# Reordering the opening of a fused linear-attention and feed-forward kernel: FFN1 of the first tokens from the first weight slice on, FFN2 of the first tokens in weight order

## The chip, the cores and the metric

The kernel runs on one core of one Trainium2 chip. The metric is device time in microseconds (us), as the median of several executions. A profile records one execution. Its span, from the first to the last instruction, is 1.7 to 2.9 us shorter than the time of the same execution. Times inside a profile count from the start of that span.

Engines: TensorE (PE in the profile; PEld is its weight loads), VectorE (DVE), ScalarE (ACT), GpSimd (POOL), and SyncE (SP), whose queue (SPq) issues the DMAs. In the traces ScalarE, VectorE and GpSimd take up their instructions in the order in which the program issues them.

## The reference

```python
# attention: B=4, H=8, S=768, D=48
for t in range(S):
    cur = einsum('bhd,bhe->bhde', u[None] * kt, vt)
    y[:, :, t] = einsum('bhd,bhde->bhe', rt, state + cur)
    state = w[None, :, :, None] * state + einsum('bhd,bhe->bhde', kt, vt)
# feed-forward on x = y as 3072 tokens x 384
h = maximum(x @ w_in, 0)          # 384 -> 2048
out = (h * h) @ w_out             # 2048 -> 384
```

## The kernel before

The sequence is cut into 24 chunks of 128 tokens, four batches times six. Two chunks make a group g of 256 tokens, so there are 12 groups. A chunk i passes through these pieces:

- `prep(i)`: scale k and r by decay powers (two products, into `rk`). `prep_du(i)`: two products for the bonus term.
- `turn(i)`: transpose `rk` into `rkT`. Chunks 0 to 3 do it on TensorE with a ScalarE copy, later chunks by a DMA transpose.
- `piece_A` (scores on TensorE, masked by VectorE into `Bm`), `bonus` (VectorE: `du`, then the product `dv`), `piece_YU` (output Y and state increment U, then state update `S0W`), `piece_X` (transpose into `xT`, the FFN input).

A group then passes through FFN1 in eight pieces s (`piece_F1`: one slice of `w_in`, relu, square) and FFN2 in eight pieces (`piece_F2`). In the steady state one period runs `piece_F1(g, s)`, `piece_F2(g-1, s)` and the attention of group g+1, woven over s = 0 to 7.

```python
    def piece_F1(g, s):
        xT = xTs[g]
        hp = psH.tile([128, 2, GT], FP32, name=f"hp_{g}_{s}", tag="H")   # psH: two buffers
        ...                                                            # six matmuls with W1[s]
        nc.scalar.activation(hr, hp, AF.Relu)
        if s % 4 == 3:
            nc.scalar.activation(hq, hr, AF.Square)
        else:
            nc.vector.tensor_mul(hq, hp, hr)          # frees hp only here

    def att(g, s):
        a = 2 * g
        b = a + 1
        if s == 0:   cast_v(a); piece_A(a); bonus(a)
        elif s == 2: cast_v(b); piece_A(b); bonus(b)
        elif s == 3: piece_YU(a)
        elif s == 4: piece_YU(b)
        elif s == 5: piece_X(a)
        elif s == 6: piece_X(b)

    def preps(g, s):
        if s == 0:   prep(2 * g, nc.gpsimd); turn(2 * g)
        elif s == 2: prep_du(2 * g, nc.gpsimd)
        elif s == 4: prep(2 * g + 1, nc.gpsimd); turn(2 * g + 1)
        elif s == 6: prep_du(2 * g + 1, nc.gpsimd)
    # (att and preps: line breaks shortened)

    for i in range(4):                        # the opening
        prep(i, nc.vector)
        prep_du(i, nc.gpsimd)
        turn(i)
        if i % 2 == 1:
            period(i // 2, None, None)        # attention of groups 0 and 1
    for s in range(NS):
        cast_w1(s)                            # all weight casts on GpSimd
    for s in range(NS):
        cast_w2(s)
    ...                                       # preps of chunks 4 and 5, loads
    period(None, 0, None)                     # FFN1 of group 0
    period(None, 1, None)                     # FFN1 of group 1
    period(2, None, 0)                        # attention of group 2 with FFN2 of group 0
    for g in range(2, NG + 1):
        period(g + 1 if g + 1 < NG else None, g if g < NG else None, g - 1)
```

## Time and profile before

| | kernel before |
|---|---|
| time, three runs | 205.73 us (205.68 to 205.82) |
| span of the profile | 203.6 us |
| first FFN1 matmul of group 0 / of group 2 | 32.8 / 61.3 us |
| periods with attention, group 3 on (mean of eight) | 13.7 us |
| last group without attention, then the FFN2 left over | 10.4 and 5.2 us |

The timeline of TensorE: start, duration (both in us), engine, line, operation, output and inputs, shape, number of instructions merged.

```profile
32.76 1.49 PE L319 MATMUL hp_0_497<-xT_315,W_0_439 128*128 128x256 bf16 x6
34.04 1.49 PE L319 MATMUL hp_1_508<-xT_315,W_1_441 128*128 128x256 bf16 x6
35.66 0.90 PE L319 MATMUL hp_2_519<-xT_315,W_2_443 128*128 128x256 bf16 x6
...
61.26 0.82 PE L319 MATMUL hp_0_832<-xT_795,W_0_439 128*128 128x256 bf16 x6
```

Six matmuls of FFN1 make one piece `hp`. The first two pieces take 1.49 us from first start to last end and the third takes 0.90. The last line shown is where the steady state begins.

The table of waits of TensorE between 61 and 184 us: who waited for whom, the sum, how often, the longest.

```profile
PE Ap_1396 L251 <- DMA rkT_1250<-rk_182: 0.9, 1, 0.9
PE Ap_1890 L251 <- DMA rkT_1744<-rk_182: 0.8, 1, 0.8
...
PE Ap_1149 L251 <- DMA rkT_1003<-rk_178: 0.5, 1, 0.5
```

There are seven such waits, each in a period of its own. TensorE stands still until the DMA transpose of the group's second chunk has landed.

Busy time by engine in four periods of the steady state (the window, its length, then PE, PEld, DVE, ACT and POOL in us with instruction counts, the granted clock, and the DMA share and rate). Each window runs from one group's first FFN1 matmul to the next.

```profile
core 0: us, PE busy (x) PEld busy (x) DVE busy (x) ACT busy (x) POOL busy (x), PEclk, DMA share, GB/s
88.15:102.13 13.98, 13.03 (x136) 9.59 (x134) 10.59 (x18) 8.43 (x17) 9.96 (x11) 1.00 0.69 152
102.13:115.84 13.71, 13.03 (x136) 9.60 (x134) 10.32 (x18) 8.43 (x17) 9.51 (x11) 1.00 0.70 154
115.84:129.73 13.89, 13.05 (x136) 9.59 (x134) 10.50 (x18) 8.43 (x17) 9.94 (x11) 1.00 0.75 141
129.73:143.38 13.65, 12.99 (x136) 9.60 (x134) 10.26 (x18) 8.44 (x17) 9.51 (x11) 1.00 0.83 159
```

### The profile page before, as it was taken

What the parts mean: (1) busy time and instruction counts of PE and PEld (TensorE: products, weight loads), DVE (VectorE), ACT (ScalarE), POOL (GpSimd) and SP (SyncE); (2) the same over time, 40 slices, a digit from 0 to 9 for tenths busy, and PEclk for the clock granted to TensorE, in tenths of its full rate; (3) what the DMA queues carried; (4) which work ended last, traced back from release to release, by engine and by line L of the source; (5) the groups of instructions that cost most, each with busy time, mean ns of one, the idle gap of its engine ahead of it and who ended that gap; (6) DMA issues with size and microseconds to landing.
All of it is one profiled execution on the core that took longest, in us unless ns stands there. A gap on an engine that the chain in (4) does not pass through costs nothing.

```text
span 203.6 us, 4241 instructions
## 1 busy us (share of the span) xinstructions
PE 168.7 (83%) x1624; PEld 123.2 (61%) x1624; DVE 133.2 (65%) x230; ACT 109.9 (54%) x203; POOL 117.8 (58%) x130
## 2 busy tenths in 40 slices
PE   0763647677959998998999989989989899999992
PEld 0643434455546776775767757767767577677761
DVE  4379793454966939849759489397595783963310
ACT  3360613657516484575574745755756657556640
POOL 2487973891856494692992965938929749100000
PEclk9999999999999999999999999999999999999999
DMA  5999999829714946929929649689499396311112
GB/s 109 208 209 279 384 351 252 223 52 192 146 40 94 207 118 142 197 77 194 219 54 210 152 109 214 96 176 207 60 210 180 92 210 120 84 42 39 39 40 79
DMA packets 105140, 31.07 MB, mean 153 GB/s; under 512 B 96672, under 2 KB 105120, under 8 KB 105120
## 3 DMA queue, kind: packets, MB, share of 16 engines
q1 hardware_dynamic: 105120, 30.81, 66.3%
q8 instruction: 12, 0.20, 0.4%
q14 instruction: 8, 0.07, 0.1%
HBM read 20.84 MB, written 4.72 MB: 126 GB/s over the span
## 4 chain that ended last, share of the span: by engine, by line
PE 25%; POOL 24%; DVE 20%; DMA 13%; SPq 8%; issue 5%; ACT 4%; ACTq 0%
SPq L83 2%; SPq L81 2%; DMA kf_1562<-in_k_dram 2%; DMA kf_2056<-in_k_dram 2%; DMA kf_1315<-in_k_dram 2%; DMA kf_1809<-in_k_dram 2%; DMA kf_1068<-in_k_dram 2%; DMA rf_110<-in_r_dram 2%; DMA vf_828<-in_v_dram 2%; POOL rk_180 L199 1%; POOL rk_178 L199 1%; POOL rk_182 L200 1%; POOL rk_178 L200 1%; POOL S0W_211 L298 1%; POOL rk_182 L199 1%
## 5 line engine op out<-in xcount | busy, mean ns | idle before, releaser
L319 PEld LDWEIGHTS <-W_0_439 128*128 128x128 bf16 x72 | 7.3, 102 | 3.0 <-issue 0.9
L319 PEld LDWEIGHTS <-W_2_443 128*128 128x128 bf16 x72 | 7.1, 99 | 3.3 <-issue 1.3
L182 PE MATMUL wl_ps<-esel,wrow 1*128 1x96 f32 x16 | 3.7, 423 | 6.5 <-ACT wrow L174 6.5
L319 PEld LDWEIGHTS <-W_6_451 128*128 128x128 bf16 x72 | 6.6, 97 | 2.6 <-issue 1.9
L319 PEld LDWEIGHTS <-W_3_445 128*128 128x128 bf16 x72 | 6.4, 97 | 2.9 <-issue 1.2
L319 PEld LDWEIGHTS <-W_4_447 128*128 128x128 bf16 x72 | 6.5, 97 | 2.4 <-issue 1.7
L319 PEld LDWEIGHTS <-W_1_441 128*128 128x128 bf16 x72 | 6.6, 102 | 2.0
L182 PEld LDWEIGHTS wl_ps<-esel,wrow 1*128 1x128 f32 x16 | 3.5, 325 | 6.5 <-ACT wrow L174 6.5
L319 PEld LDWEIGHTS <-W_7_453 128*128 128x128 bf16 x72 | 6.7, 98 | 0.7
L319 PEld LDWEIGHTS <-W_5_449 128*128 128x128 bf16 x72 | 6.5, 98 | 0.7
L199 POOL TENSOR_TENSOR rk_180<-kf_486,Wkhat 128x384 bf16<-128x384 f32 x1 | 1.0, 1007 | 4.9 <-DMA kf_486<-in_k_dram 4.9
L309 ACT COPY xT_315<-px_316 128x384 bf16<-128x384 bf16 x1 | 0.5, 479 | 6.2 <-PE px_316 L308 6.2
L309 ACT COPY xT_428<-px_429 128x384 bf16<-128x384 bf16 x1 | 0.5, 479 | 6.0 <-PE px_429 L308 6.0
L205 POOL TENSOR_TENSOR P_0_215<-rf_90,kf_91 128x384 f32<-128x384 f32 x1 | 1.4, 1366 | 4.0 <-DMA kf_91<-in_k_dram 4.0
L199 POOL TENSOR_TENSOR rk_176<-kf_821,Wkhat 128x384 bf16<-128x384 f32 x1 | 1.0, 998 | 4.6 <-DMA kf_821<-in_k_dram 4.6
L199 POOL TENSOR_TENSOR rk_180<-kf_1068,Wkhat 128x384 bf16<-128x384 f32 x1 | 1.0, 999 | 4.1 <-DMA kf_1068<-in_k_dram 4.1
L199 POOL TENSOR_TENSOR rk_180<-kf_1562,Wkhat 128x384 bf16<-128x384 f32 x1 | 1.0, 1007 | 4.0 <-DMA kf_1562<-in_k_dram 4.0
L199 POOL TENSOR_TENSOR rk_180<-kf_2550,Wkhat 128x384 bf16<-128x384 f32 x1 | 1.0, 1000 | 4.1 <-DMA kf_2550<-in_k_dram 4.1
L199 POOL TENSOR_TENSOR rk_180<-kf_2056,Wkhat 128x384 bf16<-128x384 f32 x1 | 1.0, 1002 | 4.0 <-DMA kf_2056<-in_k_dram 4.0
L199 POOL TENSOR_TENSOR rk_176<-kf_2303,Wkhat 128x384 bf16<-128x384 f32 x1 | 1.0, 1006 | 3.9 <-DMA kf_2303<-in_k_dram 3.9
L199 POOL TENSOR_TENSOR rk_176<-kf_1315,Wkhat 128x384 bf16<-128x384 f32 x1 | 1.0, 997 | 3.9 <-DMA kf_1315<-in_k_dram 3.9
L199 POOL TENSOR_TENSOR rk_176<-kf_1809,Wkhat 128x384 bf16<-128x384 f32 x1 | 1.0, 1004 | 3.8 <-DMA kf_1809<-in_k_dram 3.8
(1126 smaller groups left out, 669.7 us busy)
## 6 DMA issues: line engine op xcount, KB each, us to landing
W1f_116<-in_moe_w_in_dram SPq DMA_DIRECT2D x1, 384.0 KB, 4.8
W1f_118<-in_moe_w_in_dram SPq DMA_DIRECT2D x1, 384.0 KB, 5.1
W1f_120<-in_moe_w_in_dram SPq DMA_DIRECT2D x1, 384.0 KB, 5.8
W1f_122<-in_moe_w_in_dram SPq DMA_DIRECT2D x1, 384.0 KB, 6.2
W1f_124<-in_moe_w_in_dram SPq DMA_DIRECT2D x1, 384.0 KB, 6.8
W1f_126<-in_moe_w_in_dram SPq DMA_DIRECT2D x1, 384.0 KB, 6.6
W1f_128<-in_moe_w_in_dram SPq DMA_DIRECT2D x1, 384.0 KB, 6.8
W1f_130<-in_moe_w_in_dram SPq DMA_DIRECT2D x1, 384.0 KB, 6.7
```

Of the source, the lines that this page charges most:

```text
L81: nc.sync.dma_start(out=rf, in_=r_v[b, c])
L83: nc.sync.dma_start(out=vf, in_=v_v[b, c])
L182: nc.tensor.matmul(wl_ps[:, hc, :], wrow[:, e, hc, :], esel[:, e, :], start=(e == 0), stop=(e == 1), skip_group_check=True,)
L199: eng.tensor_mul(rk_buf[i % NB][:, 1, :, 0:D], kf, Wkhat)
L200: eng.tensor_mul(rk_buf[i % NB][:, 0, :, 0:D], rf, Wt2)
L205: eng.tensor_mul(P0, rf, kf)
L298: nc.gpsimd.tensor_mul(S0W[b], ts, WLm)
L309: nc.scalar.copy(xTs[g][:, :, L * j : L * (j + 1)], px)
L319: nc.tensor.matmul(hp[:, fi, :], W1[s][:, c, 128 * fi : 128 * (fi + 1)], xT[:, c, :], start=(c == 0), stop=(c == CCH - 1), skip_group_chec ...
```

## The change

The intent is to use TensorE's idle time in the opening. FFN1 of group 0 starts as soon as the first weight slice has arrived, woven with the attention of group 1 (chunks 2 and 3). FFN1 of group 1 is woven with the start of attention of group 2. The loads are reordered to match. The steady state changes too: the second chunk's prep comes in step 1 instead of step 4, and the loads are issued earlier.

```diff
     def cast_w1(s):
         t = const.tile([128, CCH, GT], BF16, name=f"W1_{s}")
-        nc.gpsimd.tensor_copy(t, W1f[s])
+        if s < 4:
+            nc.scalar.copy(t, W1f[s])
+        else:
+            nc.gpsimd.tensor_copy(t, W1f[s])
 ...                    # loads: 4, 5 before W2; 6, 7 after it; decay matrix WLm built another way
-        if i < 4:                       # turn: chunks 4 and 5 now also on TensorE
+        if i < 6:
 ...                    # piece_YU, state update
+            ts = work.tile([128, HP, 2 * D], FP32, name=f"ts_{i}", tag="ts")
             if c == 0:
-                nc.vector.tensor_mul(S0W[b], U, WLm)
+                nc.scalar.copy(ts, U)
             else:
-                ts = work.tile(...)
                 nc.vector.tensor_add(ts, U, S0W[b])
-                nc.gpsimd.tensor_mul(S0W[b], ts, WLm)
+            nc.gpsimd.tensor_mul(S0W[b], ts, WLm)
 ...
-        j, q = s // 4, s % 4
+        j, q = (s % 2, s // 2) if g == 0 else (s // 4, s % 4)      # FFN2 of group 0
 ...                    # preps: second chunk
-        elif s == 2:
-            prep_du(2 * g, nc.gpsimd)
-        elif s == 4:
+        elif s == 1:
             prep(2 * g + 1, nc.gpsimd)
             turn(2 * g + 1)
+        elif s == 4:
+            prep_du(2 * g, nc.gpsimd)
 ...                    # the opening, from chunk 3 on
+    turn(3)
+    for s in range(8):
+        cast_w1(s)
+        piece_F1(0, s)
+        att(1, s)
+    for s in range(8):
+        cast_w2(s)
+        if s == 0:
+            prep(4, nc.vector); prep_du(4, nc.gpsimd); turn(4)
+        if s == 2:
+            prep(5, nc.vector); prep_du(5, nc.gpsimd); turn(5)
+        piece_F1(1, s)
+        if s >= 4:
+            att(2, s - 4)
+    for s in range(4):
+        F2_next()                       # FFN2 pieces from one list, in order
+        att(2, s + 4)
+        preps(3, 2 * s)
+        ...
+    for g in range(2, NG):
+        for s in range(8):
+            piece_F1(g, s)
+            F2_next()
+            ...                         # att(g + 1, s), preps(g + 2, s)
+            if s == 3: load(2 * g + 6)
+            if s == 7: load(2 * g + 7)
+    while F2s:
+        F2_next()                       # 12 FFN2 pieces are left over instead of 8
```

More of the change, by code (lines that the diff above doesn't have):

```diff
@@ L48 @@
     stage = ctx.enter_context(tc.tile_pool(name="stage", bufs=3))
-    loads = ctx.enter_context(tc.tile_pool(name="loads", bufs=7))
+    loads = ctx.enter_context(tc.tile_pool(name="loads", bufs=8))
     work = ctx.enter_context(tc.tile_pool(name="work", bufs=3))
@@ L118 @@
         load_w1(s)
+    load(4)
+    load(5)
     for s in range(NS):
         load_w2(s)
-        if s == 3:
-            load(4)
-    load(5)
+    load(6)
+    load(7)
     tcol_i = const.tile([128, 1], mybir.dt.int32, name="tcol_i")
@@ L158 @@
         rk_buf.append(t)
-    wrow = const.tile([1, 2, HP, 128], FP32, name="wrow")
-    nc.vector.memset(wrow, 0.0)
-    esel = const.tile([1, 2, 2 * D], FP32, name="esel")
-    nc.vector.memset(esel, 0.0)
-    nc.vector.memset(esel[:, 0, 0:D], 1.0)
-    nc.vector.memset(esel[:, 1, D : 2 * D], 1.0)
+    wrow = const.tile([1, HP, 128], FP32, name="wrow")
+    nc.gpsimd.memset(wrow, 0.0)
+    one = const.tile([1, 1], FP32, name="one")
+    nc.gpsimd.memset(one, 1.0)
+    own = const.tile([128, 2 * D], FP32, name="own")
+    nc.gpsimd.memset(own, 0.0)
+    nc.gpsimd.memset(own[0:64, 0:D], 1.0)
+    nc.gpsimd.memset(own[64:128, D : 2 * D], 1.0)
     logw = const.tile([128, H, D], FP32, name="logw")
@@ L171, with make_WLm @@
     nc.scalar.activation(Wt2, logw, AF.Exp, scale=tcol)
-    logw_p = logw.rearrange("p (a e) d -> p e a d", e=2)
-    for e in range(2):
-        nc.scalar.activation(
-            wrow[:, e, :, 64 * e : 64 * e + D], logw_p[0:1, e], AF.Exp, scale=float(L)
-        )
+    nc.scalar.activation(
+        wrow.rearrange("p a (e x) -> p a e x", e=2)[:, :, :, 0:D],
+        logw.rearrange("p (a e) d -> p a e d", e=2)[0:1],
+        AF.Exp,
+        scale=float(L),
+    )
     WLm = const.tile([128, HP, 2 * D], FP32, name="WLm")
-    wl_ps = psU.tile([128, HP, 2 * D], FP32, name="wl_ps", tag="U", padded_shape=[None, None, 128])
-    for hc in range(HP):
-        for e in range(2):
+    def make_WLm():
+        ps = psU.tile([128, HP], FP32, name="wl_ps", tag="U", padded_shape=[None, 512])
+        for hc in range(HP):
             nc.tensor.matmul(
-                wl_ps[:, hc, :],
-                wrow[:, e, hc, :],
-                esel[:, e, :],
-                start=(e == 0),
-                stop=(e == 1),
-                skip_group_check=True,
-            )
-    nc.scalar.copy(WLm, wl_ps)
+                ps[:, hc : hc + 1], wrow[:, hc, :], one, start=True, stop=True, skip_group_check=True
+            )
+        wlT = const.tile([128, HP], FP32, name="wlT")
+        nc.scalar.copy(wlT, ps)
+        for hc in range(HP):
+            nc.gpsimd.tensor_scalar(WLm[:, hc, :], own, wlT[:, hc : hc + 1], None, op0=ALU.mult)
     S0W = [const.tile([128, HP, 2 * D], BF16, name=f"S0W_{b}") for b in range(B)]
@@ L292, in piece_YU @@
         if c < NCH - 1:
+            ts = work.tile([128, HP, 2 * D], FP32, name=f"ts_{i}", tag="ts")
             if c == 0:
-                nc.vector.tensor_mul(S0W[b], U, WLm)
+                nc.scalar.copy(ts, U)
             else:
-                ts = work.tile([128, HP, 2 * D], FP32, name=f"ts_{i}", tag="ts")
                 nc.vector.tensor_add(ts, U, S0W[b])
-                nc.gpsimd.tensor_mul(S0W[b], ts, WLm)
+            nc.gpsimd.tensor_mul(S0W[b], ts, WLm)
         nat.pop(i)
@@ L383, in preps @@
             turn(2 * g)
-        elif s == 2:
-            prep_du(2 * g, nc.gpsimd)
-        elif s == 4:
+        elif s == 1:
             prep(2 * g + 1, nc.gpsimd)
             turn(2 * g + 1)
+        elif s == 4:
+            prep_du(2 * g, nc.gpsimd)
         elif s == 6:
             prep_du(2 * g + 1, nc.gpsimd)
-    def period(ga, g1, g2):
-        for s in range(8):
-            if g1 is not None:
-                piece_F1(g1, s)
-            if g2 is not None:
-                piece_F2(g2, s)
-            if ga is not None:
-                att(ga, s)
-                if ga > 1:
-                    preps(ga + 1, s)
-                if s == 7 and ga > 1:
-                    load(2 * ga + 4)
-                    load(2 * ga + 5)
@@ L406 @@
-    for i in range(4):
-        prep(i, nc.vector)
-        prep_du(i, nc.gpsimd)
-        turn(i)
-        if i % 2 == 1:
-            period(i // 2, None, None)
-    for s in range(NS):
-        cast_w1(s)
-    for s in range(NS):
-        cast_w2(s)
-    for i in (4, 5):
-        prep(i, nc.gpsimd)
-        turn(i)
-        prep_du(i, nc.gpsimd)
-    load(6)
-    load(7)
-    period(None, 0, None)
-    period(None, 1, None)
-    period(2, None, 0)
-    for g in range(2, NG + 1):
-        period(g + 1 if g + 1 < NG else None, g if g < NG else None, g - 1)
+    F2s = [(g, s) for g in range(NG) for s in range(8)]
@@ new lines, in F2_next @@
+    def F2_next():
+        if F2s:
+            piece_F2(*F2s.pop(0))
+    prep(0, nc.vector)
+    prep_du(0, nc.gpsimd)
+    turn(0)
+    prep(1, nc.vector)
+    prep_du(1, nc.gpsimd)
+    turn(1)
+    cast_v(0)
+    piece_A(0)
+    bonus(0)
+    prep(2, nc.gpsimd)
+    cast_v(1)
+    piece_A(1)
+    turn(2)
+    make_WLm()
+    piece_YU(0)
+    bonus(1)
+    prep(3, nc.gpsimd)
+    piece_YU(1)
+    piece_X(0)
+    piece_X(1)
+    prep_du(2, nc.gpsimd)
+    prep_du(3, nc.gpsimd)
+    turn(3)
@@ new lines @@
+    for s in range(8):
[5 more added lines that the diff above has]
+        if s == 0:
+            prep(4, nc.vector)
+            prep_du(4, nc.gpsimd)
+            turn(4)
+        if s == 2:
+            prep(5, nc.vector)
+            prep_du(5, nc.gpsimd)
+            turn(5)
+        piece_F1(1, s)
[5 more added lines that the diff above has]
+        preps(3, 2 * s)
+        if s == 0:
+            preps(3, 1)
@@ L430 @@
+    load(8)
+    load(9)
+    for g in range(2, NG):
+        for s in range(8):
+            piece_F1(g, s)
+            F2_next()
+            if g + 1 < NG:
+                att(g + 1, s)
+                preps(g + 2, s)
+            if s == 3:
+                load(2 * g + 6)
+            if s == 7:
+                load(2 * g + 7)
+    while F2s:
+        F2_next()
 _INS = ['r', 'k', 'v', 'w', 'u', 'moe_w_in', 'moe_w_out']
```

## The prediction

> **What bounds the kernel now.** From 61.3 us (first FFN1 matmul of group 2, timeline) TensorE is the limit: the last group without attention takes 10.44 us, eight FFN1 pieces of 0.66 us and eight FFN2 pieces of 0.65 us back to back. The nine groups with attention take (184.1 - 61.3) / 9 = 13.64 us. One period summed from the timeline (115.84 to 129.73) is 13.05 us of TensorE work and 0.84 us of waiting for the transposed chunk (`Ap <- DMA rkT`). The table of waits lists that wait seven times, 5.1 us together. The opening, 0 to 61.3 us, is bound by chains across engines: loads until about 12 us, then VectorE and attention, FFN1 of groups 0 and 1 from 32.8 to 50.9 us at 1.13 us a piece, attention of group 2 mixed with FFN2 of group 0 until 61.3 us.
>
> **What the change does.**
> 1. Steady state: the second chunk's prep moves from step 4 to step 1 and its loads earlier, so the transposes land long before use. Gain about 5 us, all on TensorE's path.
> 2. Tail: only 4 FFN2 pieces lie in the opening instead of 8, so 12 instead of 8 follow the last FFN1: 4 x 0.65 = +2.6 us.
> 3. Opening: FFN1 of group 0 starts at about 24 us instead of 32.8, but in a chain. (The 16 decay matmuls, 3.7 us, go, but VectorE waits for chunk 1's load at 10.1 us anyway.) In steps 0 to 3 ScalarE casts the slice (about 0.8 us, from its 0.48 us for 384 and 1.01 us for 1024 elements), TensorE runs the piece (0.85 us with latency), ScalarE does relu (0.6 us), in two steps a v cast (0.5 us), and only then casts the next slice: 2.4 to 2.9 us a step against 1.13. In steps 4 and 5 GpSimd's cast stands in its queue behind the state update (1.0 us), which waits for ScalarE's new copy of U. I get the end of FFN1 of group 0 at 45 us (before: 42). Group 1 then shares VectorE with two preps, masks and bonus terms (about 12 us of work, with stalls), and two YU steps and transposes follow in series: group 2 starts at about 67 us.
> 4. Clock: the Trainium skill, "TensorE: Matmul & The Clock Gate" (Part 1), says that TensorE runs at half clock until it was busy for some 3.4 us; the trace agrees: the first two pieces of FFN1 have matmuls of 421 ns, from 35.7 us on 272 ns. Interleaved pieces may stay cold, up to 0.6 us each: I add 2 us, so group 2 starts at 69 us (65 to 72).
> 5. GpSimd preps chunk 6 only after the state updates: its transpose lands after group 2 has started, a wait of about 2 us once.
>
> **Sum.** Opening +7.7, wait +2, tail +2.6, steady state -5: +7.3 us, rounded down to +6.6 as terms can overlap. Predicted 212.3 us, 207.5 to 217.5. Chances: faster 0.10, same 0.20, slower 0.70.
>
> **What would show it.** First FFN1 matmul of group 2 at 65 to 72 us; ScalarE weight casts alternating with relu; FFN1 matmuls of group 0 partly at 421 ns; no `Ap <- DMA rkT` waits after the second period, periods near 13.05 us; 12 FFN2 pieces at the end (7.8 us).
>
> **What would make it wrong.** If the woven FFN1 runs faster than my chain (group 2 by 60 us), the result is same or slightly faster. If the new load order starves the steady state, it is slower still.

## More of the kernel before

Subtract the DVE column from the length: 13.98 - 10.59, 13.71 - 10.32, 13.89 - 10.50 and 13.65 - 10.26 are all 3.39 us.

In the timeline of VectorE the 3.39 us are its idle time, and nearly all of it is waiting for ScalarE's relu of pieces 0, 5 and 6.

## The result and the profile after

| | before | after |
|---|---|---|
| time, four runs each | 205.70 us (204.89 to 205.82) | 222.84 us (221.96 to 223.60) |
| span of the profile | 203.6 | 221.6 |
| first FFN1 matmul of group 0 / of group 2 | 32.8 / 61.3 | 26.0 / 73.9 |
| period of group 2 | 13.3 | 16.4 |
| the eight periods after it, together | 109.35 | 109.29 |
| FFN2 left over at the end | 5.2 | 7.8 |

The ratio is 1.084 (95% interval 1.079 to 1.089), so the change is 8.4% slower. This ratio, like every other one below, is the mean time of one kernel's fast runs over that of the other kernel's fast runs in the same rounds, so it is not quite the ratio of the medians.

The span grew by 18.0 us, and the table says where: 12.6 us before group 2 starts, 3.1 us in the period of group 2, nothing in the next eight periods, and 2.6 us in the longer tail. That makes 18.3 us; from the last matmul to the end of the span it is 0.3 us less than before.

The timeline of the first woven loop, all engines. The bracket at the end of a line is how long the engine was idle before and what ended it.

```profile
25.12 0.83 ACT L101 CAST W_0_376<-W1f_116 128x768 bf16<-128x768 f32 x1
26.01 1.46 PE L324 MATMUL hp_0_378<-xT_348,W_0_376 128*128 128x256 bf16 x6 [1.84 <-ACT W_0_376 L101]
27.51 0.60 ACT L333 ACTIVATE hr_0_385<-hp_0_378 128x512 bf16<-128x512 f32 x1 [1.55 <-PE hp_0_378 L324]
28.01 0.50 ACT L216 CAST vb_389<-vf_106 128x384 bf16<-128x384 f32 x1
28.41 0.83 ACT L101 CAST W_1_407<-W1f_118 128x768 bf16<-128x768 f32 x1
29.30 1.46 PE L324 MATMUL hp_1_409<-xT_348,W_1_407 128*128 128x256 bf16 x6 [1.28 <-ACT W_1_407 L101]
...
38.11 0.46 ACT L300 COPY ts_480<-U_473 128x384 f32<-128x384 f32 x1
38.64 0.99 POOL L303 TENSOR_TENSOR S0W_214<-ts_480,WLm 128x384 bf16<-128x384 f32 x1 [10.13 <-ACT ts_480 L300]
39.58 0.83 POOL L103 CAST W_4_483<-W1f_124 128x768 bf16<-128x768 f32 x1
40.46 1.46 PE L324 MATMUL hp_4_485<-xT_348,W_4_483 128*128 128x256 bf16 x6 [2.92 <-POOL W_4_483 L103]
```

This is the chain that the change built. ScalarE casts a slice, TensorE runs the piece, ScalarE does the relu and a v cast, and only then comes the next slice's cast. The steps start 3.3 us apart (26.01 and 29.30). From piece 4 on the casts are GpSimd's, but they stand behind the state update `S0W`, which waits for ScalarE's copy `ts`. The slice for `W_4` had landed at 23.4 us, but its cast runs only at 39.58. So `hp_4` waits 2.92 us. Each piece takes 1.46 us. Group 2 begins here:

```profile
73.89 0.81 PE L324 MATMUL hp_0_838<-xT_801,W_0_376 128*128 128x256 bf16 x6
```

The waits of TensorE over the whole span:

```profile
PE hp_4_485 L324 <- POOL W_4_483 L103: 2.9, 1, 2.9
PE Ap_855 L256 <- DMA rkT_790<-rk_192: 2.6, 1, 2.6
...
PE hp_5_517 L324 <- POOL W_5_515 L103: 2.5, 1, 2.5
...
PE hp_3_1918 L324 <- DVE hq_1_1875 L338: 0.5, 1, 0.5
```

The waits for `rkT` in the steady state are gone. One of them, `Ap_855`, is left in the period of group 2. A new small wait has come: piece 3 of FFN1 waits for VectorE's square of piece 1, because `hp` has two buffers. The line for `hp_3_1918` is one of eight of that length.

The windows of four steady periods, columns as before:

```profile
core 0: us, PE busy (x) PEld busy (x) DVE busy (x) ACT busy (x) POOL busy (x), PEclk, DMA share, GB/s
103.85:117.97 14.12, 13.09 (x136) 9.68 (x134) 10.74 (x18) 8.43 (x17) 9.97 (x11) 1.00 0.87 186
117.97:131.73 13.76, 13.09 (x136) 9.68 (x134) 10.37 (x18) 8.44 (x17) 9.77 (x11) 1.00 0.71 154
131.73:145.55 13.82, 13.10 (x137) 9.68 (x135) 10.43 (x18) 8.44 (x17) 9.76 (x11) 1.00 0.72 153
145.55:159.13 13.58, 13.09 (x135) 9.67 (x134) 10.20 (x18) 8.43 (x17) 9.76 (x11) 1.00 0.74 158
```

Length minus DVE is 3.38, 3.39, 3.39 and 3.38 us, the same as before. The chain of work that ended last, inside the third of these periods:

```profile
134.05 1.28 DVE Bm_1847 L265 x2
135.33 0.47 DVE du_1858 L222
...
135.82 0.56 DVE dv_1860 L227
136.38 0.28 DVE hq_1_1875 L338
...
136.90 0.68 DVE hq_2_1894 L338
137.58 1.20 DVE Bm_1903 L265 x2
138.77 0.47 DVE du_1914 L222
...
139.27 0.82 DVE dv_1916 L227
140.09 0.48 DVE xs_1954 L295
```

From 134 to 140.6 us the chain lies on VectorE: mask, `du` and `dv` of the first chunk, two squares of FFN1, mask, `du` and `dv` of the second chunk, then `xs`, on which the next Y waits.

### The profile page after: what moved, and what is told of

It is laid out like the page before. It is cut to its first block, busy times and chain, and to the rows that moved or that the text cites. A ratio compares the mean times of both kernels' runs of the same rounds, so it can differ in the third digit from the quotient of the medians.

```text
span 221.6 us, 4263 instructions
## 1 busy us (share of the span) xinstructions
PE 175.2 (79%) x1632; PEld 125.0 (56%) x1632; DVE 130.5 (59%) x222; ACT 115.8 (52%) x212; POOL 121.0 (55%) x139
## 4 chain that ended last, share of the span: by engine, by line
PE 39%; DVE 27%; ACT 9%; issue 8%; DMA 6%; POOL 5%; SPq 4%; ACTq 0%; POOLq 0%
SPq L83 2%; DMA rf_1328<-in_r_dram 2%; DMA rf_110<-in_r_dram 1%; DMA rkT_790<-rk_192 1%; DMA rf_971<-in_r_dram 1%; PE o_3161 L349 1%; PE o_3141 L349 1%; PE o_3121 L349 1%; PE o_3068 L349 1%; PE o_3004 L349 1%; SPq L82 1%; PE o_988 L349 1%; PE o_2223 L349 1%; PE o_2914 L349 1%; PE o_1235 L349 1%
## 5 line engine op out<-in xcount | busy, mean ns | idle before, releaser
L324 PEld LDWEIGHTS <-W_3_451 128*128 128x128 bf16 x72 | 7.4, 104 | 7.9 <-issue 4.2
L324 PEld LDWEIGHTS <-W_2_420 128*128 128x128 bf16 x72 | 7.5, 105 | 4.1 <-ACT W_2_420 L101 1.9
L324 PEld LDWEIGHTS <-W_4_483 128*128 128x128 bf16 x72 | 6.9, 104 | 4.8 <-POOL W_4_483 L103 3.1
L324 PEld LDWEIGHTS <-W_0_376 128*128 128x128 bf16 x72 | 7.2, 101 | 4.2 <-ACT W_0_376 L101 2.1
L324 PEld LDWEIGHTS <-W_1_407 128*128 128x128 bf16 x72 | 6.7, 104 | 4.2 <-ACT W_1_407 L101 1.5
L324 PEld LDWEIGHTS <-W_5_515 128*128 128x128 bf16 x72 | 6.6, 101 | 3.7 <-POOL W_5_515 L103 2.7
L303 POOL TENSOR_TENSOR S0W_212<-ts_757,WLm 128x384 bf16<-128x384 f32 x1 | 1.0, 997 | 13.3 <-DVE ts_757 L302 13.3
L324 PEld LDWEIGHTS <-W_7_552 128*128 128x128 bf16 x72 | 6.9, 101 | 2.2 <-issue 1.2
L324 PEld LDWEIGHTS <-W_6_534 128*128 128x128 bf16 x72 | 6.9, 102 | 1.4 <-issue 0.5
L238 PE MATMUL pt_222<-identity,rk_188 128*128 128x128 bf16 x8 | 1.2, 308 | 7.4 <-DVE rk_188 L204 6.8
L238 PEld LDWEIGHTS <-rk_188 128*128 128x128 bf16 x16 | 1.1, 114 | 9.9 <-DVE rk_188 L204 8.1
L303 POOL TENSOR_TENSOR S0W_214<-ts_480,WLm 128x384 bf16<-128x384 f32 x1 | 1.0, 994 | 10.1 <-ACT ts_480 L300 10.1
L238 PEld LDWEIGHTS <-rk_190 128*128 128x128 bf16 x16 | 1.4, 130 | 7.0 <-DVE rk_190 L204 5.3
L338 DVE TENSOR_TENSOR hq_0_387<-hp_0_378,hr_0_385 128x512 bf16<-128x512 f32 x1 | 0.7, 693 | 7.3 <-ACT hr_0_385 L333 7.3
L195 POOL TENSOR_SCALAR WLm<-own,wlT 128x96 f32<-128x96 f32 x4 | 2.2, 560 | 3.4 <-ACT wlT L193 3.4
L324 PE MATMUL hp_4_485<-xT_348,W_4_483 128*128 128x256 bf16 x6 | 1.5, 416 | 2.9 <-POOL W_4_483 L103 2.9
L238 PE MATMUL pt_615<-identity,rk_190 128*128 128x128 bf16 x8 | 1.2, 307 | 3.0 <-DVE rk_190 L204 2.5
L338 DVE TENSOR_TENSOR hq_4_494<-hp_4_485,hr_4_492 128x512 bf16<-128x512 f32 x1 | 0.7, 692 | 4.8 <-ACT hr_4_492 L333 4.8
L324 PE MATMUL hp_5_517<-xT_348,W_5_515 128*128 128x256 bf16 x6 | 1.5, 416 | 2.5 <-POOL W_5_515 L103 2.5
L238 PE MATMUL pt_238<-identity,rk_190 128*128 128x128 bf16 x8 | 1.2, 306 | 2.8 <-DVE rk_190 L204 2.1
L204 DVE TENSOR_TENSOR rk_188<-kf_91,Wkhat 128x384 bf16<-128x384 f32 x1 | 0.6, 558 | 4.3 <-ACT Wt_208 L177 4.3
```

The source lines that it names most:

```text
L195: nc.gpsimd.tensor_scalar(WLm[:, hc, :], own, wlT[:, hc : hc + 1], None, op0=ALU.mult)
L204: eng.tensor_mul(rk_buf[i % NB][:, 1, :, 0:D], kf, Wkhat)
L238: nc.tensor.transpose(pt[:, j, hc, :], src[:, j, 2 * hc : 2 * hc + 2, :].rearrange("p a b -> p (a b)"), identity,)
L303: nc.gpsimd.tensor_mul(S0W[b], ts, WLm)
L324: nc.tensor.matmul(hp[:, fi, :], W1[s][:, c, 128 * fi : 128 * (fi + 1)], xT[:, c, :], start=(c == 0), stop=(c == CCH - 1), skip_group_chec ...
```

## The experiments

Each kernel ran in three rounds against the kernel before on the same chip. "Ratio" is against the kernel before. The times given are medians of all four executions of a run; the ratios use the fast ones alone (o1, c2 and s6 each had one slow execution). The start of group 2 is read from each profile. The 95% intervals of the ratios reach 0.4 to 0.8% to either side.

### What held the opening

**o1: the weight casts ahead of the loop.**

```diff
     for s in range(8):
         cast_w1(s)
+    for s in range(8):
         piece_F1(0, s)
         att(1, s)
```

> The changed kernel, but all eight W1 casts (four on ScalarE, four on GpSimd) stand ahead of the loop that weaves FFN1 of group 0, none inside it. Theory 'queue chains' (the woven FFN1 is slow because each slice is cast only after the relu of the piece before it, and from slice 4 on only after the state update): FFN1 of group 0 ends 7 to 10 us earlier than its 49.5 us, group 2 starts at 64 to 67 us instead of 73.9, total 213 to 216 us. Rival 'half clock' (the pieces are slow because TensorE is cold, 1.46 us each): pieces stay at 1.46 us and the total falls by no more than 3 us, 220 or more.

Measured: 212.8 us, ratio 1.032. Group 2 starts at 63.4 us instead of 73.9. (The profiled execution was the slowest of the four, 214.9 us, so this start is rather late.) Moving the casts brings back about 10 us, a little more than expected. Not all of it is the queues: TensorE now works 5.4 us without a pause at the start of the loop, and the pieces of group 0 take 0.82 us from the fourth on. Of the 16 woven pieces 7 are slow (about 1.45 us), against 12 in the changed kernel. I estimate the clock's share at 5 x 0.64 = 3.2 us.

**o2: the first state update on VectorE, as before.**

```diff
             if c == 0:
-                nc.scalar.copy(ts, U)
+                nc.vector.tensor_mul(S0W[b], U, WLm)
             else:
                 ...
-            nc.gpsimd.tensor_mul(S0W[b], ts, WLm)
+                nc.gpsimd.tensor_mul(S0W[b], ts, WLm)
```

> The changed kernel, but the first state update is one VectorE multiply straight from U, as before the change, so no ScalarE copy and no GpSimd update stand ahead of a cast. Theory 'queue chains': the two waits of FFN1 pieces 4 and 5 for their casts (2.9 and 2.5 us in the changed kernel) shrink to under 1 us each, total 3 to 5 us less (218 to 220). Rival 'half clock': at most 1 us less.

Measured: 217.1 us, ratio 1.055, 5.7 us less than the changed kernel by the medians, a little more than expected. Here too 7 pieces are slow instead of 12, so a part of the gain is the clock's. The two waits for W slices 4 and 5 are gone from the table of waits. The start of FFN1 moved from 26.0 to 28.1 us, because VectorE now waits for the late `WLm`. Group 2 starts at 66.3 us.

**o3: TensorE kept busy with matmuls of constants.**

```diff
+    def warm(n):
+        for _ in range(n):
+            nc.tensor.matmul(warm_ps[:, 0:128], identity, maskJT, start=True, stop=True, ...)
 ...
         piece_F1(0, s)
         att(1, s)
+        warm((12, 12, 8, 24, 20, 0, 0, 8)[s])      # and some before turn(3), turn(5), in the second loop
```

> The changed kernel with 128-column matmuls of constants, whose result nobody reads, put into TensorE's waits of the opening, nothing else changed. Theory 'half clock': FFN1 matmuls of groups 0 and 1 take 272 ns instead of 421, pieces 0.8 us instead of 1.46, and group 2 starts 4 to 7 us earlier: total 216 to 219. Rival 'queue chains alone': pieces get faster but the casts and preps set the pace, total within 2 us of 222.8.

Measured: 216.9 us, ratio 1.055. Group 2 starts at 67.0 us, 6.9 us earlier. The timeline of the first pieces (in this profile the names carry no numbers):

```profile
25.88 0.84 PE L324 MATMUL hp<-xT,W 128*128 128x256 bf16 x6
...
26.98 0.84 PE L407 MATMUL warm_ps<-maskJT,identity 128*128 128x128 bf16 x12
28.54 0.83 PE L324 MATMUL hp<-xT,W 128*128 128x256 bf16 x6 [0.72 <-ACT W L101]
```

With useless work in its gaps, a piece takes 0.84 us instead of 1.46, in all but the last of the 16 pieces. The matmuls of a piece start 0.11 us apart instead of 0.21, which is half the pace. So both rivals have a part: the clock alone costs some 6 us here, and o1 brought back more than its estimated share of the clock. The gains are not additive, since a faster piece also shortens the chain in which the casts stand, and casts that come earlier also leave fewer slow pieces.

**c1: all three together.**

> The changed kernel with casts hoisted, state update on VectorE and the constant matmuls together. If the three causes are the whole of what the woven opening lost, group 2 starts near the 61.3 us of the kernel before (59 to 63) and the total is 208 to 212 (the first-period wait of 2.6 to 3 us and the longer tail of 2.6 us stay). If something else holds the opening, group 2 starts after 64 us.

Measured: 216.0 us, ratio 1.051, group 2 at 65.2 us. This missed the expectation, and the result is worse than o1 alone. The timeline shows one reason: the first FFN1 piece starts at 28.8 us instead of 26.0, because the update on VectorE waits for `WLm` (two waits of TensorE for `S0W`, 2.4 and 1.4 us). With the casts hoisted, it seems that moving the update to VectorE has nothing left to gain; no run takes it out of c1 alone. From the last FFN1 piece of group 0 (43.1 us) to group 2 it still took 22 us, so a cause was missing from the list.

**o7: chunks 4 and 5 off VectorE.** This is o1 with:

```diff
-        if i < 6:                          # turn: by DMA again
+        if i < 4:
-            prep(4, nc.vector)             # and the same for chunk 5
+            prep(4, nc.gpsimd)
```

> o1_casts_hoisted with chunks 4 and 5 prepped on GpSimd and transposed by DMA as in the kernel before, instead of VectorE, TensorE, FFN1's PSUM banks and ScalarE. Theory 'the second loop is held by the preps and their transposes in the FFN1 queues': FFN1 of group 1, 22 us from first piece to group 2 in the changed kernel's repaired form, takes 16 to 18 us, total 206.5 to 209 against 212.4. Rival 'attention of group 2 itself holds it': total 211 or more.

Measured: 210.1 us, ratio 1.024, group 2 at 59.6 us. This fell between the two expectations. From the first FFN1 piece of group 1 to group 2 it takes 20.0 us (o1: 21.3), not 16 to 18. FFN1 of group 1 now runs quickly up to its piece 4, then TensorE waits for a DMA:

```profile
48.69 0.61 PE L256 MATMUL Ap<-rkT 48*128 48x128 bf16 x8 [3.77 <-DMA rkT<-rk]
```

The `rk` of chunk 4 was ready at 40.8 us, but its transpose was issued only at 45.0 us, because the queue of SyncE had the loads of chunks 6 and 7 ahead of it (until 44.8 us). One wait went and another came.

### What sets the steady state

The theory is that VectorE's queue sets the period in both kernels. The rival is the prediction, in which the wait for the transposes lies on TensorE's critical path.

**s1: the steady-state part of the change alone, on the kernel before** (the new `preps`, one load in step 3 and one in step 7, eight load buffers).

> The kernel before, with only the steady-state part of the change: prep of the second chunk in step 1, one load in step 3 and one in step 7, one more load buffer. The recorded prediction's step 1: the waits for the transposes go and the periods fall to about 13.05 us, total about 200.5 us. Theory 'VectorE sets the period' (in both traces the period minus VectorE's busy time is 3.38 to 3.39 us in every one of the six middle periods): the waits for the transposes go, TensorE waits for hq of piece 1 instead (about 0.5 us), total 204.5 to 206.5.

Measured: 206.5 us, ratio 1.002 (0.997 to 1.008), the same as before. Its table of waits has nine waits for the square `hq` (4.1 us together) and none for `rkT`. The prediction's step, that these waits alone are worth 5 us, is refuted.

**s2 and s3: one VectorE square less per period, without and with that part.**

```diff
-        if s % 4 == 3:
+        if s % 4 == 3 or (s == 1 and g > 1):
             nc.scalar.activation(hq, hr, AF.Square)
```

> The kernel before, but from group 2 on the square of FFN1 piece 1 goes to ScalarE, as pieces 3 and 7 already do, so VectorE has 0.69 us less per period. Theory 'two limits in turn': VectorE's queue sets the period, and the wait for the transposes (0.5 to 0.9 us) lies just beneath it; with VectorE relieved the transposes hold the period, total falls by 0 to 2 us (203.5 to 205.8). Rival 'VectorE alone': every period falls by 0.6 to 0.7 us, total 199.5 to 201.

Measured: 204.5 us, ratio 0.996, as the first theory says.

> The kernel before with the steady-state part of the change and the same relief of VectorE together. Theory 'two limits in turn': now both limits are gone, the periods fall to 13.05 to 13.2 us, total 199.5 to 202. Rival 'the early prep is worth nothing': no better than s2_before_dve_relieved.

Measured: 204.1 us, ratio 0.994. This missed: s3 is no better than s2. Its windows show why (columns as before; the windows of this and the next runs go from one group's first attention matmul to the next, 1.4 us after its first FFN1 matmul):

```profile
89.87:103.36 13.49, 13.03 (x136) 9.60 (x136) 10.11 (x17) 9.07 (x18) 10.10 (x11) 1.00 0.73 156
103.36:117.63 14.27, 13.04 (x136) 9.59 (x136) 10.88 (x17) 9.06 (x18) 9.83 (x11) 1.00 0.72 150
131.18:144.29 13.11, 13.04 (x135) 9.60 (x135) 9.72 (x17) 9.07 (x18) 10.09 (x11) 1.00 0.72 147
```

Length minus DVE is still 3.38 to 3.39, so VectorE still holds the period, but its busy time did not fall by 0.69. The product `dv` took 0.56 to 1.32 us. What was taken away came back as stretch.

**s6 and s9: where the stretch comes from (wrong results).** In the traces before and after, from 60 us on, every `dv` that takes longer than 0.56 us overlaps a GpSimd product. The Trainium skill, "GPSIMD Engine Reference" (1. Specifications), says that GpSimd shares its SBUF interfaces with VectorE, with contention for VectorE instructions in a two-port mode or with two SBUF inputs. `dv` is such an instruction (two SBUF inputs). `hq` and `xs` read PSUM in one input and keep their 0.68 and 0.55 us.

```diff
     def prep_du(i, eng):
+        if i > 5:
+            du_in[i] = ub
+            return
```

> Wrong result on purpose: s3_steady_part_dve_relieved in which GpSimd leaves out the two products of the bonus term from chunk 6 on (VectorE reduces a constant tile instead, same instructions), so GpSimd has 4 us less per period. Theory 'GpSimd stretches VectorE': the stretched products of VectorE (0.56 us alone, up to 1.3 us beside GpSimd) mostly return to 0.56, periods 13.0 to 13.2, total 199.5 to 202. Rival 'the stretch has another source': periods stay near 13.5, total 203.5 to 205.

Measured: 202.9 us, ratio 0.988. The periods average 13.4 us. This missed, because the wrong half of GpSimd's work was taken away. The preps now meet `dv`:

```profile
107.67 1.00 POOL L200 TENSOR_TENSOR rk<-rf,Wt 128x384 bf16<-128x384 f32 x1
107.84 1.25 DVE L225 TENSOR_TENSOR dv<-vf,du 128x384 f32<-128x384 f32 x1
```

The two lines also show the size of the stretch: the GpSimd product ends at 108.67 us and `dv` at 109.09, 0.42 us later. In all runs together 117 `dv` after 60 us are stretched, and 116 of them end 0.41 to 0.42 us after the end of the GpSimd product that was running when they began. So `dv` behaves as if it waited for that product.

s9 drops those preps as well, from chunk 8 on:

> Wrong result on purpose: s6_no_bonus_product_wrong_result in which GpSimd also leaves out the preps from chunk 8 on (stale buffers are transposed), so that from group 3 on only the state updates are left on GpSimd. Theory 'GpSimd stretches VectorE': every dv product takes 0.56 us, VectorE is busy 9.56 us a period and the period is 9.56 + 3.39 = 12.95 us. Rival: dv still takes up to 1.3 us and periods reach 13.5 to 13.8.

Measured: 199.1 us, ratio 0.970. Every `dv` takes 0.56 us and every full period is 12.92 to 12.96 us, as computed in advance. The windows:

```profile
75.56:88.52 12.96, 12.96 (x137) 9.53 (x136) 9.56 (x17) 9.06 (x18) 2.00 (x2) 1.00 0.77 163
101.47:114.42 12.95, 12.95 (x137) 9.52 (x136) 9.56 (x17) 9.05 (x18) 2.00 (x2) 1.00 0.77 163
```

VectorE is busy 9.56 us in each of them, and the periods no longer vary. (TensorE is shown busy all the time here too, so both limits now nearly meet. But TensorE is not what holds 12.95: in s4, below, it gets through a period in 12.74 us.)

**s4 and s5: two squares less on VectorE, with and without the early prep.**

```diff
-        if s % 4 == 3:
+        if s % 4 == 3 or (s in (1, 2) and g > 1):
```

> The kernel before with the steady-state part of the change, and the squares of FFN1 pieces 1 and 2 (from group 2 on) on ScalarE: 1.37 us less VectorE work per period than s1_steady_part_alone. Theory 'VectorE's busy time plus 3.39 us is the period until TensorE's 13.05 us holds': mean period 12.9 to 13.2, total 198.5 to 201.5. Rival 'VectorE is not the limit': no better than the 204.1 of s3_steady_part_dve_relieved.

Measured: 200.4 us, ratio 0.978 (0.973 to 0.983). Two of its periods:

```profile
76.71:89.45 12.74, 12.74 (x135) 9.53 (x134) 9.12 (x16) 9.69 (x19) 10.07 (x11) 1.00 0.77 165
89.45:102.86 13.41, 13.04 (x137) 9.61 (x136) 9.77 (x16) 9.71 (x19) 10.08 (x11) 1.00 0.74 158
```

In the first one TensorE is busy all the time, 12.74 of 12.74 us, so the 13.05 us that the prediction and this expectation took for TensorE's work is not its floor. In the second one VectorE's busy time is 0.65 us longer, and the period is 0.67 us longer.

> The kernel before with only the squares of FFN1 pieces 1 and 2 moved to ScalarE (no early prep). Theory 'two limits in turn': the waits for the transposes now hold the period near 13.6, total 203 to 205, so the early prep of the change is what makes the 200.4 us of s4_steady_dve_relieved_twice possible. Rival 'the early prep is worth nothing': total 200 to 201.5, as s4.

Measured: 204.4 us, ratio 0.993 (0.986 to 1.000). The line of its table of waits:

```profile
PE Ap L251 <- DMA rkT<-rk: 6.7, 7, 1.2
```

Without the early prep, the wait for the transposes holds the period at 13.6 to 13.9 us. One and the same step shows the turn. The mask of the second chunk needs the scores `Ap` that wait for the transpose. Before, VectorE still has a queue of work then and takes up the mask without a pause; in s5 it stands idle until `Ap` comes:

```profile
121.96 1.27 DVE L260 TENSOR_TENSOR Bm_1891<-Ap_1890,maskJT 128x512 bf16<-128x512 f32 x2
...
108.35 1.29 DVE L260 TENSOR_TENSOR Bm<-Ap,maskJT 128x512 bf16<-128x512 f32 x2 [0.82 <-PE Ap L251]
```

(The first line is from the kernel before, the second from s5.) The mean of the periods of groups 3 to 8 is 13.77 us before, 13.69 with the early prep alone (s1), 13.72 with the relief alone (s5) and 12.96 with both (s4). The two limits stood almost level. So the early prep is worth 3 to 4 us (by the ratios and by the medians), but only once VectorE has been relieved. By itself it is worth nothing (s1), and relief by itself is worth about 1 us (s2, s5).

### Putting it together

**c2**: c1 with the preps of chunks 6 and 7 in the second loop and one square relieved.

> c1_opening_repaired with the preps of chunks 6 and 7 ahead of the state updates of chunks 4 and 5 in GpSimd's queue, and the relief of VectorE from group 2 on. The wait for the transpose of chunk 6 (2.6 us) goes and the periods fall to about 13.1 us: total 200 to 204 us, about the time of the kernel before. Theory 'VectorE does not set the period': only the 2.6 us come back, 206 to 209.

Measured: 208.8 us, ratio 1.014, so slower than expected; the time lies in the range of the rival, 206 to 209. The wait of group 2 for its transpose went (its period is 13.3 us instead of 17.1 in c1), but the periods stayed at 13.4 on average. Yet length minus DVE is 3.38 to 3.39 us in each of the six middle periods, so this does not speak for the rival: the relief of one square was given back as stretch, as in s3.

**b2**: the changed kernel with the casts ahead, constant matmuls, chunks 4 and 5 as in o7, chunks 6 and 7 as in c2, and two squares relieved.

> The changed kernel with casts hoisted, constant matmuls, chunks 4 and 5 on GpSimd and DMA, chunks 6 and 7 prepped ahead of the state updates, and the squares of pieces 1 and 2 on ScalarE from group 2 on. If the causes named are the whole: group 2 starts at 57 to 61 us, no first-period wait, periods near 13.1, total 197.5 to 202, the fastest of all. If it is over 203, a cause is missing.

Measured: 200.3 us, ratio 0.977 (0.969 to 0.985). Group 2 starts at 59.2 us, and the periods average 12.9. This is as fast as s4, which keeps the old opening: the repaired woven opening gains 2.1 us against the 61.3 us of the kernel before and pays 2.6 us in the tail.

**b3**: b2 with the preps and transposes of chunks 4 and 5 in the first woven loop, the loads of chunks 6 and 7 after them.

> b2_all_repairs with the preps and transposes of chunks 4 and 5 moved into the first woven loop and the loads of chunks 6 and 7 issued after them. If the new wait of o7 and b2 for the transpose of chunk 4 (3.8 and 2.6 us) is what still holds the second loop: group 2 starts 2 to 4 us before b2's 59.2 us, total 196.5 to 198.5. If attention of group 2 on VectorE holds it, the total stays within 1 us of b2's 200.3.

Measured: 198.5 us, ratio 0.956 (0.950 to 0.962), the fastest correct kernel. The kernel before took 206.9 us in its rounds, so the ratio counts here. The reason I gave is not confirmed. The wait for the transpose is gone, but in the profiled execution (the slowest of its four, 199.3 us) group 2 starts at 59.0 us, no earlier than in b2. Waits for VectorE (`hq`, `xs`, `Bm`) stand in its place. The profile of b2 is of its fastest execution (199.1 us), so the two profiled executions take the same time and can't show the difference. Where the 2% against b2 came from stays open.

## Why the prediction was wrong

The direction was right (slower, with 0.70). The size was not: predicted +6.6 us, measured +17.1 us by the medians, outside the range of 207.5 to 217.5. Term by term, in spans:

| term | predicted | measured | |
|---|---|---|---|
| opening | +7.7 (group 2 at 69, range 65 to 72) | +12.6 (73.9) | too small |
| wait in group 2's period | +2 | +3.1 (one wait of 2.6) | right in kind |
| tail | +2.6 | +2.6 | right |
| steady state | -5 | -0.06 | wrong |

- **"Steady state: ... Gain about 5 us, all on TensorE's path."** This is the step whose reason failed, and with it the opening line "From 61.3 us ... TensorE is the limit". The waits for the transposes were real, and they did go. But removing them gained next to nothing (0.06 us over eight periods, not 5). VectorE's queue set the period, with a constant 3.39 us besides its busy time, and TensorE's wait lay just beneath that. When the wait went, piece 3 of FFN1 waited for VectorE instead. s1 shows that the part is worth nothing by itself, s9 that the period is 9.56 + 3.39 us when VectorE is undisturbed, and s4 against s5 what it is worth once VectorE is no longer the limit. The numbers were there beforehand: subtracting VectorE's busy time from the periods of the kernel before would have pointed to it.
- **"Interleaved pieces may stay cold ...: I add 2 us."** The mechanism was right, but this term of the sum was mis-sized. Twelve of the 16 woven pieces of groups 0 and 1 ran with matmuls of about 420 ns for most or all of their length (in the profile, the eight of group 0, the last one only mostly, and four of group 1). o3, which only keeps TensorE busy, brings group 2 forward by 6.9 us.
- **"2.4 to 2.9 us a step"** and "behind the state update": right. The steps start 3.3 us apart where a cold piece and a v cast meet, the chain is visible line by line, and o1 and o2 remove it. My warm estimate for group 2's start, 67 us, is just what o3 shows with a warm clock (67.0 us), and its end of FFN1 of group 0, 45 us, is met there too (44.6).
- **Tail and first wait**: both were seen as named.

Of the 10.7 us by which the span grew more than the sum of +7.3, 4.9 are the steady state, 4.9 the opening and 1.1 the wait (less 0.3 at the very end).

So the woven opening could not pay as written. It started FFN1 6.8 us earlier but finished the first group at 49.5 us, while the kernel before finished it at about 42. Even with every named cause repaired, the opening itself gained only some 2 us.

## What to carry to other kernels

A wait on the busiest engine is worth something only if no other engine's queue sets the pace. Before you price it, take several periods and see which engine's busy time the period follows one to one. When you weave early work into a stage full of dependencies, put its preparation (casts, copies, transposes, loads) ahead of the loop and not inside it, because each in-order queue turns program order into a chain. Remember that a sparse stream of matmuls may run at half clock (here 1.46 us a piece instead of 0.84).

## What the Trainium skill lacked or had wrong

- "TensorE: Matmul & The Clock Gate" ("Why this matters for your kernels") advises against idle gaps over some 3 us and gives no share of busy time below which an interleaved stream falls back to half clock. In the changed kernel the matmuls ran at full pace from 49.1 us and were slow again from about 52.4, with no wait of TensorE longer than 1.1 us between. Before that, from 26.0 to 45.0 us, all pieces were slow (matmuls of about 420 ns), and no unbroken run of TensorE was longer than 2.1 us; the first longer run, 4.4 us from 45.0 on, ended at 272 ns. In the kernel before, 272 ns followed on a run of 3.0 us. In o1 matmuls were still slow 4.8 us into a run of 5.4. The share of work that keeps the clock up stays open.
- The same page warns that clock events in traces are unreliable (Part 1, "Seeing it yourself"). The window of the changed kernel's first woven loop shows a granted clock of 1.00 (the third number from the end) while its matmuls take about 420 ns:

```profile
26.00:49.50 23.50, 14.07 (x94) 9.02 (x94) 9.59 (x17) 9.40 (x18) 10.41 (x13) 1.00 0.90 231
```

- A measured time for the contention between GpSimd and VectorE (it belongs to "GPSIMD Engine Reference", 1. Specifications, and no page has it for such a pair of products). Here a 128x384 fp32 product with two SBUF inputs takes 0.56 us alone and up to 1.4 us beside GpSimd products, ending 0.41 to 0.42 us after the product that was running when it began. This moved whole periods, from 13.1 to 14.3 us in s3.
